# A fused retention and two-MoE kernel: decode scratch and activation sum of the first unit moved into PSUM, scores moved inside the first layer

## Chip, cores and metric

The kernel runs on one NeuronCore of a Trainium2 chip. The metric is device time in microseconds, from the first to the last instruction with what lies around it; three runs of the kernel before gave 1019.86, 1021.78 and 1024.08 us.

## What is computed

Three stages follow each other. A retention layer (4 batches, 8 heads, 768 tokens, head size 64, a decaying state per head) gives 3072 token rows of 512 values. A dense layer follows, and then a routed mixture of 8 experts:

```python
state = gamma * state + k_t v_t^T ;  y_t = scale * q_t state        # retention
h = x @ w_in
g = np.maximum(h, 0.0) + np.log1p(np.exp(-np.abs(h)))               # softplus
x = g @ w_out                                                       # 512 -> 2048 -> 512
e = argmax(x @ w_gate); out = x + prob_e * relu(x @ w1[e]) @ w2[e]  # where x @ w_skip > 0
```

All inputs are float32; `w_in` and `w_out` arrive as 64-bit words (a float64 each), and the kernel turns each word's two halves into one float32 by integer operations.

## The kernel before, in words

TensorE multiplies in a format with fewer bits than float32, so every factor is split into `hi` (rounded) and `lo` (the rest), and each product is three matmuls: hi by hi, lo by hi, hi by lo.

**Units and steps.** The 3072 tokens are 8 units T of 384. A unit has 16 steps f, one for each 128 of the 2048 hidden columns; s = 16 T + f counts all steps. The engines' queues hold the instructions in program order, which the source writes out by hand in the loop at line 748. In step s:

- scores of the next unit's retention, one pair of heads and one chunk of 128 tokens (`attn_a`, L373, TensorE) and their masking (`attn_m`, L379, VectorE);
- `mm1(T, f)` (L518): 12 matmuls, 384 columns each, into one PSUM bank *hp*; there are two such banks, so step s+1 writes the bank of step s-1;
- `act_a(T, f)` on ScalarE: Abs of *hp* (L529), Exp (L530), in unit 0 two Identity passes (L532, L533; in later units one VectorE pass, L543), and Ln (L534); from unit 1 on also a Relu of *hp* (L537);
- `attn_b`: retention sums into the bank *y* (L394, L396), state sums into columns of the bank *wps* (L403), update of the state (L411, VectorE);
- `dec_fin`: for a decoded block, ScalarE copies it to `hi` (L331), SP issues a load of a raw block three further on, POOL subtracts for `lo` (L333);
- `act_p`: two POOL additions (L545, L546);
- `act_hi` of step s-1: VectorE adds (L556 in unit 0, L554 later) to give `g`, ScalarE rounds it to `hi` (L557); one decode pass; `act_lo` of step s-1: VectorE subtracts (L563); again `dec_fin`;
- at the last chunk of a pair of heads, `attn_out` turns *y* into `xth` (L421, ScalarE) and `xtl` (L422, VectorE);
- `mm2` of step s-2 (L575): nine matmuls, 512 columns each, into three accumulators.

**Decode.** The dense weights are 32 blocks (16 of `w_in`, 16 of `w_out`), decoded during unit 0 only. A block takes three VectorE passes over 128x512 words: shift and mask (L312), or in the sign (L316), or in the low half's top bits (L320). `dec(n)` issues the next n passes. Ten blocks are decoded before the steps begin, together with unit 0's own retention; the other 66 passes lie in steps 0 to 15: two in step 0, one in step 1, then 4 and 5 in turn.

**PSUM.** Eight banks: two *hp*, three accumulators, and one each tagged `sc`, `y` and `wps`. In the kernel before, head 0's scores go to `sc` and head 1's to columns 256 to 383 of `wps`.

Of the kernel before, what the change touches and what calls it, by code (L numbers as in the profile page):

```python
# [7 lines left out]
F32 = mybir.dt.float32  # L8
F32R = mybir.dt.float32r
BF16 = mybir.dt.bfloat16  # L10
I32 = mybir.dt.int32
AF = mybir.ActivationFunctionType
ALU = mybir.AluOpType
# [8 lines left out]
TT = 384  # L22
# [3 lines left out]
KD = DM // 128  # L26
# [45 lines left out]
def retention_moe_moe2(ctx: ExitStack, tc: tile.TileContext, a: dict, out: bass.AP):  # L72
    nc = tc.nc
# [9 lines left out]
    ps_s = ctx.enter_context(tc.tile_pool(name="ps_s", bufs=1, space=PSUM))  # L83
# [187 lines left out]
    with tc.manual_schedule():  # L271
        with ExitStack() as p1:
# [3 lines left out]
            at1 = p1.enter_context(tc.tile_pool(name="at1", bufs=1))  # L276
            at2 = p1.enter_context(tc.tile_pool(name="at2", bufs=2))
            gp2 = p1.enter_context(tc.tile_pool(name="gp2", bufs=2))
            mp = p1.enter_context(tc.tile_pool(name="mp", bufs=2))
# [6 lines left out]
            wps = ps_s.tile([128, 512], F32, name="wps")  # L286
# [18 lines left out]
            def decode():  # L305
                for n, (f, side) in enumerate(blocks):
                    w = wo[:, f] if side else wi[:, f].rearrange("p t k n -> p t (k n)")
                    hi, lo = w[:, 0, :], w[:, 1, :]
                    raw = raws[n].rearrange("p (n two) -> p n two", two=2)
                    lw, hw = raw[:, :, 0], raw[:, :, 1]  # L310
                    m = mp.tile([128, 512], I32, name="m")
                    nc.vector.tensor_scalar(  # L312
                        out=m, in0=hw, scalar1=0x07FFFFFF, scalar2=3, op0=ALU.bitwise_and, op1=ALU.logical_shift_left,
                    )
                    yield
                    nc.vector.scalar_tensor_tensor(  # L316
                        out=m, in0=hw, scalar=-0x40000000, in1=m, op0=ALU.bitwise_and, op1=ALU.bitwise_or,
                    )
                    yield
                    nc.vector.scalar_tensor_tensor(  # L320
                        out=m, in0=lw, scalar=29, in1=m, op0=ALU.logical_shift_right, op1=ALU.bitwise_or,
                    )
                    ready.append((m, hi, lo))
                    yield
# [10 lines left out]
            def dec(n):  # L335
                for _ in range(n):
                    next(steps, None)
# [26 lines left out]
            def attn_a(U, p, c, dst=None, am=None):  # L364
                s = st[U, p]
                cs = slice(c * 128, (c + 1) * 128)
                if dst is None:
                    sc = ps_s.tile([128, 512], F32, name="sc")
                    dst = (sc[:, 0:128], wps[:, 256:384])
                    am = at1.tile([128, 256], F32, name="am")  # L370
                for h in range(2):
                    hs = slice(h * 64, (h + 1) * 64)
                    nc.tensor.matmul(dst[h], lhsT=s["kt"][hs, cs], rhs=s["qt"][hs, cs], start=True, stop=True)  # L373
                s["am", c] = am, dst

            def attn_m(U, p, c):
                am, dst = st[U, p]["am", c]
                for h in range(2):
                    nc.vector.scalar_tensor_tensor(  # L379
                        out=am[:, h * 128:(h + 1) * 128], in0=dst[h], scalar=cst[:, C_MS + 2 * p + h:C_MS + 2 * p + h + 1], in1=mask,  # L380
                        op0=ALU.mult, op1=ALU.mult,
                    )

            def attn_b(U, p, c, dw=None):
                s = st[U, p]
                cg = (U % 2) * CPU + c
                cs = slice(c * 128, (c + 1) * 128)
                if dw is None:
                    dw = wps[:, 0:D]
                    if c == 0:  # L390
                        s["y"] = ps_s.tile([128, 512], F32, name="y")[:, 0:TT]
                y, (am, _) = s["y"], s.pop(("am", c))
                if cg:
                    nc.tensor.matmul(y[:, cs], lhsT=wsb[p], rhs=s["qt"][:, cs], start=True, stop=False)  # L394
                for h in range(2):
                    nc.tensor.matmul(  # L396
                        y[h * 64:(h + 1) * 64, cs], lhsT=nat(s["vn"], c, h), rhs=am[:, h * 128:(h + 1) * 128],
                        start=(cg == 0), stop=True,
                    )
                if cg < S // 128 - 1:  # L400
                    for h in range(2):
                        hs = slice(h * 64, (h + 1) * 64)
                        nc.tensor.matmul(dw[hs], lhsT=nat(s["kn"], c, h), rhs=nat(s["vn"], c, h), start=True, stop=True)  # L403
                    for h in range(2):
                        hs = slice(h * 64, (h + 1) * 64)
                        if cg == 0 and U == 0:
                            nc.scalar.activation(out=wsb[p][hs, hs], in_=dw[hs], func=AF.Copy)
                        elif cg == 0:
                            nc.vector.tensor_copy(wsb[p][hs, hs], dw[hs])
                        else:  # L410
                            nc.vector.scalar_tensor_tensor(  # L411
                                out=wsb[p][hs, hs], in0=wsb[p][hs, hs], scalar=cst[hs, C_DEC + p:C_DEC + p + 1], in1=dw[hs],
                                op0=ALU.mult, op1=ALU.add,
                            )
# [11 lines left out]
            seq = [(p, c) for p in range(NP) for c in range(CPU)]  # L426
# [83 lines left out]

            gh, gl = {}, {}

            def mm1(T, f):
                hp = ps_h.tile([128, 512], F32, name="hp")[:, 0:TT]
                n = 0
                for w, x in ((0, xth[T]), (1, xth[T]), (0, xtl[T])):
                    for kk in range(KD):
                        nc.tensor.matmul(  # L518
                            hp, lhsT=wi[:, f, w, kk, :], rhs=x[:, kk, :], start=(n == 0), stop=(n == 3 * KD - 1),
                        )  # L520
                        n += 1
                gl[T, f] = hp

            def act_a(T, f):
                hp = gl[T, f]
                u = gp2.tile([128, TT], F32, name="u")
                ln = gp2.tile([128, TT], F32, name="ln")
                t = at1.tile([128, TT], F32, name="t")
                nc.scalar.activation(out=u, in_=hp, func=AF.Abs)  # L529
                nc.scalar.activation(out=u, in_=u, func=AF.Exp, scale=-1.0)  # L530
                if T == 0:
                    nc.scalar.activation(out=t, in_=u, func=AF.Identity, bias=1.0)  # L532
                    nc.scalar.activation(out=t, in_=t, func=AF.Identity, bias=io8[:, 7:8])  # L533
                nc.scalar.activation(out=ln, in_=u, func=AF.Ln, bias=1.0)  # L534
                g = gp2.tile([128, TT], F32, name="g")
                if T:
                    nc.scalar.activation(out=g, in_=hp, func=AF.Relu)  # L537
                gl[T, f] = u, ln, t, g, hp
# [10 lines left out]
            def act_hi(T, f):  # L549
                g, ln, hp = gl[T, f]  # L550
                hi = gp3.tile([128, TT], F32R, name="hi")
                gl[T, f] = g, ln
                if T:
                    nc.vector.tensor_tensor(out=g, in0=g, in1=ln, op=ALU.add)  # L554
                else:
                    nc.vector.scalar_tensor_tensor(out=g, in0=hp, scalar=0.0, in1=ln, op0=ALU.max, op1=ALU.add)  # L556
                nc.scalar.activation(out=hi, in_=g, func=AF.Copy)  # L557
                gh[T, f] = hi

# [173 lines left out]
            NS = NU * NF  # L733
# [14 lines left out]
            for s in range(NS + 2):  # L748
                T, f = divmod(s, NF)
                U = T + 1  # L750
                i = f - 2 if U < NU and 2 <= f < 2 + len(seq) else None
                if f >= 14 and U + 1 < NU:
                    attn_first(U + 1, f - 14)
                if s == 2 * NF:
                    init_records()
                if s == 1:
                    attn_a(U, *seq[0])
                    attn_m(U, *seq[0])
                if i is not None:
                    if s != 2:  # L760
                        attn_a(U, *seq[i])
                        attn_m(U, *seq[i])
                    if i % CPU == 1 and i + CPU < len(seq):
                        attn_scale_q(U, i // CPU + 1)
                dec(3+s%2 if s > 1 else (2, 0)[s])
                if s < NS:
                    mm1(T, f)
                for fn in todo.get(s + 0.5, []):
                    fn()
                if f == 0 and 1 < U < NU:  # L770
# [46 lines left out]
        with ExitStack() as left:  # L817
# [194 lines left out]
            for m, (ns, nb) in enumerate(PAIRS):  # L1012
                s, b = vis[ns], vis[nb]
# [48 lines left out]
            with tc.For_i(0, nv, 1) as it:  # L1062
                s = {"n": 0, "nb": 4, "xg": xgb[0]}
# [51 lines left out]
```

## Time and profile before

| | |
|---|---|
| median of three runs | 1021.78 us (1019.86 to 1024.08) |
| the profiled execution | 1020.42 us, its span 1018.3 us |
| TensorE busy | 962.4 us (95%) |
| VectorE, ScalarE, POOL busy | 584.7, 482.4, 563.1 us |
| mean granted TensorE clock | 0.97 of full speed |

In the profile PE is TensorE's matmuls, PEld its weight loads, DVE VectorE, ACT ScalarE, SP the engine that issues DMAs. L518 is line 518 of the kernel. A row "out<-in" names the tiles by the program's names. A releaser, after "<-", is what the waiting instruction waited for last.

### The profile page before, as it was taken

The numbers are of one execution on the slowest core, as the hardware profiler recorded it, in microseconds if no ns is written. First come the engines' busy times: TensorE is split into PE (matmuls) and PEld (weight loads), VectorE is DVE, ScalarE is ACT, GpSimd is POOL, SyncE is SP. The second block draws the span as 40 slices with busy tenths as digits, with TensorE's granted clock in tenths as the row PEclk, the third lists the DMA queues.
The fourth block names the chain that finished last, engine by engine and source line by source line (L and its number), as shares of the span: only waits on it lengthen the run. The fifth ranks groups of instructions, "written<-read, shape, count | busy, mean of one in ns | idle before, by whom it ended". The sixth has DMA issues, their size and how long they took to land.

```text
span 1018.3 us, 15594 instructions
## 1 busy us (share of the span) xinstructions
PE 962.4 (95%) x5558; PEld 802.9 (79%) x5558; DVE 584.7 (57%) x1260; ACT 482.4 (47%) x915; POOL 563.1 (55%) x455
## 2 busy tenths in 40 slices
PE   7888989999999999999999999999797999999994
PEld 6667768888888888888888888888685878797883
DVE  6899995455444644544454454446435375556743
ACT  1265565455354544544553554455453365354640
POOL 4567776545645654555465365446462673546642
PEclk8699999999999999999999999999897999999998
DMA  8535342112111212111121112001027294557710
GB/s 284 182 94 172 123 136 88 37 32 99 45 55 32 94 32 62 64 56 39 32 93 40 55 63 63 1 1 63 1 82 270 76 346 144 216 165 240 248 66 20
DMA packets 59424, 102.15 MB, mean 100 GB/s; under 512 B 9026, under 2 KB 35810, under 8 KB 59344
## 3 DMA queue, kind: packets, MB, share of 16 engines
q1 hardware_dynamic: 54432, 90.57, 26.9%
q0 software_dynamic: 4048, 8.85, 2.5%
q10 hardware_dynamic: 864, 1.70, 0.4%
q8 instruction: 45, 0.74, 0.3%
q14 instruction: 35, 0.29, 0.1%
HBM read 85.18 MB, written 17.85 MB: 101 GB/s over the span
## 4 chain that ended last, share of the span: by engine, by line
PE 80%; DVE 12%; issue 4%; ACT 2%; DMA 1%; POOL 1%; SPq 0%; ACTq 0%; POOLq 0%; DVEq 0%
PE hp L518 25%; PE ac L575 24%; PE op L902 9%; PE hp L862 8%; DVE m L316 3%; PE sc L373 3%; PE y L396 3%; PE hp L876 2%; DVE m L312 2%; DVE m L320 1%; PE y L394 1%; DVE lo L563 1%; PE tp L600 1%; PE hp L172 1%; DVE wsb L411 1%
## 5 line engine op out<-in xcount | busy, mean ns | idle before, releaser
L545 POOL TENSOR_TENSOR ln<-ln,t 128x384 f32<-128x384 f32 x127 | 151.4, 1192 | 255.6 <-ACT ln L534 125.9
L575 PE MATMUL ac<-wo,hi 128*128 128x512 f32 x768 | 272.5, 409 | 6.1 <-ACT hi L557 6.1
L518 PE MATMUL hp<-xth,wi 128*128 128x384 f32 x1024 | 215.5, 353 | 9.2 <-DVE g L556 8.4
L518 PEld LDWEIGHTS hp<-xth,wi 128*128 128x128 f32 x1024 | 177.6, 190 | 23.4 <-DVE g L556 10.2
L529 ACT ACTIVATE u<-hp 128x384 f32<-128x384 f32 x128 | 62.7, 490 | 250.3 <-PE hp L518 234.3
L575 PEld LDWEIGHTS ac<-wo,hi 128*128 128x128 f32 x768 | 145.1, 189 | 43.8 <-ACT hi L557 7.2
L546 POOL TENSOR_TENSOR ln<-ln,u 128x384 f32<-128x384 f32 x127 | 152.8, 1204 | 10.0
L575 PE MATMUL ac<-wo,lo 128*128 128x512 f32 x384 | 151.8, 395 | 0.8 <-DVE lo L563 0.7
L563 DVE TENSOR_TENSOR lo<-g,hi 128x384 fp32r<-128x384 f32 x128 | 97.5, 762 | 68.2 <-ACT hi L557 67.0
L518 PE MATMUL hp<-xtl,wi 128*128 128x384 f32 x512 | 112.8, 342 | 0.0
L156 POOL TENSOR_TENSOR l<-raw,h 128x1024 fp32r<-128x1024 f32 x30 | 77.3, 2588 | 54.7 <-ACT h L153 32.1
L543 DVE TENSOR_SCALAR t<-u 128x384 f32<-128x384 f32 x112 | 44.0, 393 | 98.2 <-ACT u L530 95.7
L411 DVE SCALAR_TENSOR_TENSOR wsb<-wsb,cst,wps 64x64 f32<-64x64 f32 x128 | 35.8, 279 | 102.9 <-PE wps L403 101.9
L518 PEld LDWEIGHTS hp<-xtl,wi 128*128 128x128 f32 x512 | 93.2, 191 | 0.0
L156 DVE TENSOR_TENSOR l<-raw,h 128x1024 fp32r<-128x1024 f32 x42 | 77.1, 1863 | 14.3 <-ACT h L153 13.8
L575 PEld LDWEIGHTS ac<-wo,lo 128*128 128x128 f32 x384 | 72.8, 190 | 14.0 <-DVE lo L563 2.6
L557 ACT ACTIVATE hi<-g 128x384 fp32r<-128x384 f32 x128 | 67.1, 524 | 34.3 <-DVE g L554 17.6
L153 ACT ACTIVATE h<-raw 128x1024 fp32r<-128x1024 f32 x71 | 72.7, 1057 | 10.0 <-PE hp L876 3.9
L530 ACT ACTIVATE u<-u 128x384 f32<-128x384 f32 x128 | 67.2, 525 | 4.1
L534 ACT ACTIVATE ln<-u 128x384 f32<-128x384 f32 x128 | 67.2, 525 | 3.5
L554 DVE TENSOR_TENSOR g<-g,ln 128x384 f32<-128x384 f32 x112 | 61.8, 552 | 0.9 <-POOL ln L546 0.9
L902 PE MATMUL op<-h,gh 128*128 128x512 f32 x152 | 59.9, 394 | 0.0
(200 smaller groups left out, 1545.6 us busy)
## 6 DMA issues: line engine op xcount, KB each, us to landing
raw<-in_moe_w SPq DMA_DIRECT2D x72, 512.0 KB
raw<-in_moe_w_out SPq DMA_DIRECT2D x16, 512.0 KB
raw<-in_moe_w_in SPq DMA_DIRECT2D x15, 512.0 KB
kn<-in_qkv SPq DMA_DIRECT2D x32, 192.0 KB
vn<-in_qkv SPq DMA_DIRECT2D x32, 192.0 KB
kt<-in_qkv SPq DMA_DIRECT2D x31, 192.0 KB
qt<-in_qkv SPq DMA_DIRECT2D x31, 192.0 KB
x1d<-x SPq DMA_DIRECT2D x21, 256.0 KB
```

The lines of the kernel that those rows point to most:

```text
L153: nc.scalar.activation(out=h, in_=r, func=AF.Copy)
L156: eng.tensor_tensor(out=lo, in0=r, in1=h.bitcast(F32), op=ALU.subtract)
L518: nc.tensor.matmul(hp, lhsT=wi[:, f, w, kk, :], rhs=x[:, kk, :], start=(n == 0), stop=(n == 3 * KD - 1),)
L530: nc.scalar.activation(out=u, in_=u, func=AF.Exp, scale=-1.0)
L534: nc.scalar.activation(out=ln, in_=u, func=AF.Ln, bias=1.0)
L545: eng.tensor_tensor(out=ln, in0=ln, in1=t, op=ALU.subtract)
L546: eng.tensor_tensor(out=ln, in0=ln, in1=u, op=ALU.add)
L557: nc.scalar.activation(out=hi, in_=g, func=AF.Copy)
L563: nc.vector.tensor_tensor(out=lo, in0=g, in1=gh[T, f].bitcast(F32), op=ALU.subtract)
L575: nc.tensor.matmul(ac[T, j], lhsT=x[:, js], rhs=wo[:, f, w, :], start=(f == 0 and n == 0), stop=(f == NF - 1 and n == 2),)
L862: nc.tensor.matmul(hp2[(2 * i + g) % 4][:, 0:w], lhsT=wt[:, kk, g * 128:(g + 1) * 128], rhs=x[:, kk, 0:w], start=(n == 0 and kk == 0), sto ...
L902: nc.tensor.matmul(op, lhsT=s[x][:, f, js], rhs=s[w, f // 2][:, f % 2, :], start=(f == 0 and n == 0), stop=(f == NF2 - 1 and n == 2),)
```

## The change

In the first two passes of a decode the words lie in the PSUM bank `sc` (new tile `x`); only the third pass writes the SBUF tile `m`. In unit 0 the sum `g` is written over *hp* in its bank, and `hi` and `lo` read it from there. While unit 0 is worked on, head 0's scores go to the columns of `wps` that head 1's had, and head 1's to columns 384 to 511 of the bank of `y`, which is claimed with the scores; their matmuls are issued after the eighth of the twelve matmuls of `mm1`, and the masking after all twelve. The decode passes of a step are dealt out anew: two before `mm1`, one or two behind it (three in step 0, none in step 1), one between `act_hi` and `act_lo`.

```diff
@@ -308,17 +308,18 @@
                     hi, lo = w[:, 0, :], w[:, 1, :]
                     raw = raws[n].rearrange("p (n two) -> p n two", two=2)
                     lw, hw = raw[:, :, 0], raw[:, :, 1]
-                    m = mp.tile([128, 512], I32, name="m")
+                    x = ps_s.tile([128, 512], I32, name="mx", tag="sc")
                     nc.vector.tensor_scalar(
-                        out=m, in0=hw, scalar1=0x07FFFFFF, scalar2=3, op0=ALU.bitwise_and, op1=ALU.logical_shift_left,
+                        out=x, in0=hw, scalar1=0x07FFFFFF, scalar2=3, op0=ALU.bitwise_and, op1=ALU.logical_shift_left,
                     )
                     yield
                     nc.vector.scalar_tensor_tensor(
-                        out=m, in0=hw, scalar=-0x40000000, in1=m, op0=ALU.bitwise_and, op1=ALU.bitwise_or,
+                        out=x, in0=hw, scalar=-0x40000000, in1=x, op0=ALU.bitwise_and, op1=ALU.bitwise_or,
                     )
                     yield
+                    m = mp.tile([128, 512], I32, name="m")
                     nc.vector.scalar_tensor_tensor(
-                        out=m, in0=lw, scalar=29, in1=m, op0=ALU.logical_shift_right, op1=ALU.bitwise_or,
+                        out=m, in0=lw, scalar=29, in1=x, op0=ALU.logical_shift_right, op1=ALU.bitwise_or,
                     )
                     ready.append((m, hi, lo))
                     yield
@@ -364,6 +365,12 @@
             def attn_a(U, p, c, dst=None, am=None):
                 s = st[U, p]
                 cs = slice(c * 128, (c + 1) * 128)
+                if U == 1:
+                    if c == 0:
+                        s["yt"] = ps_s.tile([128, 512], F32, name="y")
+                        s["y"] = s["yt"][:, 0:TT]
+                    dst = (wps[:, 256:384], s["yt"][:, 384:512])
+                    am = at1.tile([128, 256], F32, name="am")
                 if dst is None:
                     sc = ps_s.tile([128, 512], F32, name="sc")
                     dst = (sc[:, 0:128], wps[:, 256:384])
@@ -387,7 +394,7 @@
                 cs = slice(c * 128, (c + 1) * 128)
                 if dw is None:
                     dw = wps[:, 0:D]
-                    if c == 0:
+                    if c == 0 and U != 1:
                         s["y"] = ps_s.tile([128, 512], F32, name="y")[:, 0:TT]
                 y, (am, _) = s["y"], s.pop(("am", c))
                 if cg:
@@ -510,7 +517,7 @@
 
             gh, gl = {}, {}
 
-            def mm1(T, f):
+            def mm1(T, f, mid=None):
                 hp = ps_h.tile([128, 512], F32, name="hp")[:, 0:TT]
                 n = 0
                 for w, x in ((0, xth[T]), (1, xth[T]), (0, xtl[T])):
@@ -519,6 +526,8 @@
                             hp, lhsT=wi[:, f, w, kk, :], rhs=x[:, kk, :], start=(n == 0), stop=(n == 3 * KD - 1),
                         )
                         n += 1
+                        if n == 2 * KD and mid is not None:
+                            mid()
                 gl[T, f] = hp
 
             def act_a(T, f):
@@ -532,7 +541,7 @@
                     nc.scalar.activation(out=t, in_=u, func=AF.Identity, bias=1.0)
                     nc.scalar.activation(out=t, in_=t, func=AF.Identity, bias=io8[:, 7:8])
                 nc.scalar.activation(out=ln, in_=u, func=AF.Ln, bias=1.0)
-                g = gp2.tile([128, TT], F32, name="g")
+                g = gp2.tile([128, TT], F32, name="g") if T else hp
                 if T:
                     nc.scalar.activation(out=g, in_=hp, func=AF.Relu)
                 gl[T, f] = u, ln, t, g, hp
@@ -553,7 +562,7 @@
                 if T:
                     nc.vector.tensor_tensor(out=g, in0=g, in1=ln, op=ALU.add)
                 else:
-                    nc.vector.scalar_tensor_tensor(out=g, in0=hp, scalar=0.0, in1=ln, op0=ALU.max, op1=ALU.add)
+                    nc.vector.scalar_tensor_tensor(out=g, in0=g, scalar=0.0, in1=ln, op0=ALU.max, op1=ALU.add)
                 nc.scalar.activation(out=hi, in_=g, func=AF.Copy)
                 gh[T, f] = hi
 
@@ -753,18 +762,22 @@
                     attn_first(U + 1, f - 14)
                 if s == 2 * NF:
                     init_records()
-                if s == 1:
-                    attn_a(U, *seq[0])
-                    attn_m(U, *seq[0])
+                mid = seq[0 if s == 1 else i] if s == 1 or T == 0 and s > 2 and i is not None else None
                 if i is not None:
-                    if s != 2:
+                    if T:
                         attn_a(U, *seq[i])
                         attn_m(U, *seq[i])
                     if i % CPU == 1 and i + CPU < len(seq):
                         attn_scale_q(U, i // CPU + 1)
-                dec(3+s%2 if s > 1 else (2, 0)[s])
-                if s < NS:
+                if T == 0:
+                    dec(2)
+                if mid is not None:
+                    mm1(T, f, lambda: attn_a(U, *mid))
+                    attn_m(U, *mid)
+                elif s < NS:
                     mm1(T, f)
+                if T == 0:
+                    dec(1 + s % 2 if s > 1 else (3, 0)[s])
                 for fn in todo.get(s + 0.5, []):
                     fn()
                 if f == 0 and 1 < U < NU:
```

## Rows read from the trace of the kernel before

**Rows 1.** the page's slices of the span: VectorE, tenths busy:

```profile
DVE  6899995455444644544454454446435375556743
```

**Rows 2.** busy time by stretches: us busy, (x) instructions, granted clock, DMA:

```profile
100.00:125.00 25.00, 22.59 (x123) 17.40 (x121) 24.28 (x38) 14.29 (x28) 18.29 (x15) 1.00 0.42 133
```

**Rows 3.** chain of waits from 45 to 157 us, shares by line:

```profile
by line: DVE m L316 19.9%; issue 16.6%; DVE m L312 13.1%; DVE lo L563 11.4%; DVE m L320 9.3%; PE hp L518 5.6%; DVE am L379 5.4%; DVE g L556 4.9%; DVE wsb L411 3.7%; PE ac L575 1.9%; DVE xtl L422 1.8%; ACT hi L557 1.5%; ACT wo L331 1.1%; ACT
```

**Rows 4.** VectorE by line, 45 to 157 us: count, busy us, mean ns, idle before:

```profile
L320 DVE SCALAR_TENSOR_TENSOR m<-raw,m 128x512 int32<-128x512 int32 x23 | 24.2, 1050 | 0.5
L316 DVE SCALAR_TENSOR_TENSOR m<-raw,m 128x512 int32<-128x512 int32 x23 | 24.1, 1048 | 0.5
L563 DVE TENSOR_TENSOR lo<-g,hi 128x384 fp32r<-128x384 f32 x15 | 19.9, 1326 | 1.4 <-ACT hi L557 1.4
L312 DVE TENSOR_SCALAR m<-raw 128x512 int32<-128x512 int32 x23 | 17.4, 757 | 0.0
L556 DVE SCALAR_TENSOR_TENSOR g<-hp,ln 128x384 f32<-128x384 f32 x16 | 8.8, 553 | 0.2
```

**Rows 5.** timeline, POOL and VectorE: start us, us long, engine, line:

```profile
104.64 1.19 POOL L545 TENSOR_TENSOR ln<-ln,t 128x384 f32<-128x384 f32 x1
...
104.89 1.37 DVE L563 TENSOR_TENSOR lo<-g,hi 128x384 fp32r<-128x384 f32 x1
```

**Rows 6.** instructions of L312 and L316, whole span: ns min/median/max, first and last start:

```profile
L312 DVE TENSOR_SCALAR m<-raw x32: 410/456/1479, 7.8 to 149.1; 128x512 int32<-128x512 int32 x32
...
L316 DVE SCALAR_TENSOR_TENSOR m<-raw,m x32: 674/965/1670, 8.4 to 150.4; 128x512 int32<-128x512 int32 x32
```

**Rows 7.** instructions of L422, whole span:

```profile
L422 DVE TENSOR_TENSOR xtl<-y,xth x30: 543/546/558, 22.5 to 668.3; 128x384 fp32r<-128x384 f32 x30
```

**Rows 8.** timeline, ScalarE:

```profile
57.58 0.49 ACT L529 ACTIVATE u<-hp 128x384 f32<-128x384 f32 x1 [1.54 <-PE hp L518]
...
60.21 0.62 ACT L331 ACTIVATE wo<-m 128x512 fp32r<-128x512 f32 x1
...
64.25 0.49 ACT L529 ACTIVATE u<-hp 128x384 f32<-128x384 f32 x1 [2.45 <-PE hp L518]
...
133.91 0.49 ACT L529 ACTIVATE u<-hp 128x384 f32<-128x384 f32 x1 [1.98 <-PE hp L518]
...
143.98 0.63 ACT L331 ACTIVATE wo<-m 128x512 fp32r<-128x512 f32 x1 [1.16 <-DVE m L320]
144.52 0.51 ACT L557 ACTIVATE hi<-g 128x384 fp32r<-128x384 f32 x1
...
148.54 0.49 ACT L529 ACTIVATE u<-hp 128x384 f32<-128x384 f32 x1 [3.52 <-PE hp L518]
...
159.40 0.49 ACT L529 ACTIVATE u<-hp 128x384 f32<-128x384 f32 x1 [2.26 <-PE hp L518]
```

**Rows 9.** timeline of step 9, TensorE and ScalarE:

```profile
103.79 1.68 PE L518 MATMUL hp<-xth,wi 128*128 128x384 f32 x8
...
106.26 0.49 ACT L529 ACTIVATE u<-hp 128x384 f32<-128x384 f32 x1 [1.97 <-PE hp L518]
```

**Rows 10.** chain of waits in the second unit: start us, us:

```profile
161.39 0.30 PE sc L373
...
161.81 2.31 PE hp L518 x12
...
173.01 2.32 PE hp L518 x12
```

**Rows 11.** VectorE by line, before the steps (0 to 45 us):

```profile
L316 DVE SCALAR_TENSOR_TENSOR m<-raw,m 128x512 int32<-128x512 int32 x9 | 10.6, 1174 | 0.3
```

**Rows 12.** timeline, TensorE:

```profile
54.55 1.71 PE L518 MATMUL hp<-xth,wi 128*128 128x384 f32 x8 [2.19 <-DVE g L556]
...
144.56 2.69 PE L518 MATMUL hp<-xth,wi 128*128 128x384 f32 x8 [2.04 <-DVE g L556]
```

**Rows 13.** busy time by stretches, around the later gap:

```profile
146.00:148.00 2.00, 2.00 (x7) 2.00 (x7) 1.97 (x3) 0.00 (x0) 1.92 (x2) 0.50 0.13 47
```

## The prediction, made before any run of the change

> **What bounds the kernel now.** I read the slices of the page first. VectorE stands at 9 tenths from about 75 to 150 us and at 4 to 6 over most of the rest [rows 1]. The change touches little but the first unit (16 steps, about 45 to 157 us), so I went there with the stretches: of 25 us VectorE is busy 24.28, TensorE 22.59, ScalarE 14.29, POOL 18.29, and the granted clock is full [rows 2]. The chain of waits says the same: between 45 and 157 us most of the path is VectorE's decoding (L312, L316, L320), L563 and its other passes; TensorE's L518 has 5.6% [rows 3]. VectorE bounds this unit.
>
> Why it is so full is in the groups of VectorE by line. The three decode passes and `lo` take 757 to 1326 ns on average, while L556, which has one input in PSUM and one in SBUF, takes 553 [rows 4]. The timeline shows what stretches them: L563 begins at 104.89, in the middle of a POOL addition (104.64 to 105.83), and ends 0.43 us after it, having taken 1.37 us [rows 5]. Left alone, an L316 takes 0.674, its minimum [rows 6], and an L422, a subtraction of the same size as L563 but with one input in PSUM, takes 543 to 558 in all of its 30 instances, beside POOL or not [rows 7]. Waiting for POOL is the extra time, and it falls on passes with two SBUF inputs and on L312.
>
> **What the change takes from VectorE.** `x` in PSUM leaves L316 and L320 one SBUF input; `g` in PSUM does the same for L563. Priced as L316's minimum and as L422: 23 L316 save 0.37 each, 8.6 us; 23 L320 likewise 8.6; 15 L563 save 0.78 each, 11.7. L556 stays at 553, its output merely going to PSUM. L312 keeps its SBUF input but writes PSUM, which no row shows: its own extremes, 0.410 and 1.479 [rows 6], are the bounds, and I leave it at its mean of 757 since POOL is unchanged. VectorE so drops by about 29 us: at 24.28 of 25 [rows 2] it had some 109 us in the unit's 112, now 80, or 5.0 us for each of 16 steps. If it set the pace, that would be a large gain.
>
> **What takes its place.** The step is bound to the *hp* bank. There are two, so `mm1(s+1)` writes the one that step s-1 used. Before, the last reader of that bank was `g` of step s-1 (L556). Now `g` lies in the bank, and the last readers are `hi` (L557, ScalarE) and then `lo` (L563, VectorE). ScalarE works in order, and `hi` of s-1 is issued behind the whole of `act_a(s)`, which waits for the end of `mm1(s)`, and behind one decode copy. So a loop closes: mm1(s), five activations, a copy, `hi`, `lo`, mm1(s+1). Its length comes from rows, counted from the start of Abs (L529):
> - Abs to the copy: 57.58 to 60.21, 2.63 us [rows 8];
> - copy to `hi`: 143.98 to 144.52, 0.54 [rows 8]; `hi` itself 0.51;
> - `lo` as L422: 0.55 [rows 7]. mm1(s+1) can begin 4.23 us after Abs(s);
> - mm1 to the next Abs: 103.79 to 106.26, 2.47 [rows 9];
> - the scores, now in the middle of mm1 where they lie inside this loop: from L373 to L518, 161.39 to 161.81, 0.42 [rows 10].
>
> The loop is 7.12 us. Before, Abs runs from 64.25 (step 3) to 133.91 (step 13), 6.97 a step [rows 8]. What is late next is thus ScalarE's order. VectorE hides inside: per step some 5.0 us against 7.12, its decode passes done while the activations run.
>
> *The moved parts* I cost at nothing else. The 66 decode passes stay 66, two ahead of mm1, one or two behind it, one between `g` and `lo`; one copy stands ahead of `hi` in every step to 14, the second of the even steps behind it. The scores no longer wait for the state update L411 of the step before. Head 1's share `y`'s bank now: at the first chunk of a pair (steps 5, 8, 11) they wait for L422 of the step before, which follows `hi`, at times a copy, and `xth`, and should end some 1.2 us into mm1, when the scores come about 1.6 in (8 of 12 matmuls in 2.47 [rows 9]); 0 to 0.3 us if not. Behind L379, which follows two decode passes, the attention sums and `mm2` are queued on TensorE. By the busy share that leaves about 0.7 us to spare ahead of mm1(s+1): attention 1.2 and mm2 2.3 in 4.23. POOL's decode subtraction and two additions, some 1.2 to 1.3 each (one is 1.19 [rows 5]), follow the copy of s-1 and end about when Abs(s) starts; `hi` needs `g` three us later. SP's raw loads follow the copy as before.
>
> **The sum**, against the profiled execution's own time of 1020.42 us (its span is 1018.3), which is 1.36 under the median of 1021.78:
> - *Before the steps* (to 45 us): 9 L316 at 1174 ns [rows 11] could save 0.50 each, 4.4 us. ScalarE, TensorE and POOL are also on this path, so the bounds are 0 and 4.4; I take -2.0. The Trainium skill (VectorE: DVE Perf Modes, "Why PSUM operands drop a tier") says that a PSUM operand holds an fp32 pass to one element per cycle; an L312 would then be as slow as a lone L316, by that page an estimate of up to 0.28 more for each of the ten here, and the sum would be up to 2.8 us higher. No run so far shows it.
> - *Steps 0 to 2*: mm1(2) started at 54.55 after a gap of 2.19, waiting for `g` [rows 12]. mm1(1) had ended at 52.36; with Abs(1) some 0.4 behind that, because a decode copy is now in front of it, plus 4.23, mm1(2) starts at about 57.0: +2.4. At the least `hi` and `lo` come on top, +1.1. A longer gap also costs clock: after 2.04 us without work, mm1(15) ran from 144.56 to its Abs at 148.54, 3.98 instead of 2.47 [rows 8, 12], at a granted 0.50, the lower of the two levels, 1.2 against 2.4 GHz [rows 13]. Here mm1(2) took 3.03 already, so between -0.6 and +0.95; I take +0.5. Together +2.9.
> - *Step 2 to 3*: 57.58 to 64.25 is 6.67 [rows 8], now 7.12: +0.45.
> - *Steps 3 to 13*: ten times 7.12 against 69.66: +1.6.
> - *Steps 13 to 17*: 133.91 to 159.40, 25.49 [rows 8]. Now 6.70 and 6.70 (no scores), 6.16 (no copy), and about 5.5 where the next unit leaves two activations out: 25.06. TensorE has gaps of some 2 us here, as the one that lost the clock, so I put one loss of 1.5 in again: +1.1.
>
> Sum: -2.0 + 2.9 + 0.45 + 1.6 + 1.1 = **+4.0**. From step 17 on TensorE's own work sets the steps [rows 10], and nothing there is changed, so the shift stays to the end. Against the median: 1021.78 + 4.0 = **1025.8 us**, 0.4% up. A measurement of this kernel tells about 0.5%, 5.1 us, from no change, so the likeliest outcome is no clear difference, leaning to slower: 29 us of VectorE are freed and a longer hand-over eats them.
>
> **Rivals.**
> *A, VectorE's relief sets the pace (faster).* If the bank's later release were hidden, TensorE would bound the unit as it does the next one, where mm1 runs from 161.81 to 173.01 in two steps, 5.6 each [rows 10]. Eleven steps at 1.37 less give -15, and with the start's 2.0 about 1005. For it: the 24.28 of 25. Against: ScalarE's order in the rows leaves `hi` no way ahead of act_a(s). 0.08.
> *B, the clock falls inside the steps (slower).* TensorE's waits, now spread over the step, become one gap in front of each mm1. I work out 0.7 us, and as much in a step was idle at full clock before (2.41 of 25 us [rows 2]), but a gap of 2 us cost the clock [rows 12, 13]. If attention and mm2 finish earlier than I think, or the loop is longer, mm1 runs at half clock: 1.5 us a time. Four to six falls give +10 to +13, 1032 to 1035. [...] 0.15.
> *C, the change does not relieve VectorE.* Decode passes in PSUM still wait for POOL, or take longer there. Then VectorE (7 us a step) and the loop meet, and `lo` is late: 0.3 to 0.6 us a step, +3 to +7 on top, 1029 to 1033. Against: L556 and L422 never stretched [rows 4, 7]. 0.15.
> Forecast: 0.62.
>
> **How the numbers follow.** With all terms at their better ends (start -4.4, steps 0 to 2 at +1.1, no lost clock) the sum is -1.7 or 1020; a reading 1.5 us lower from the spread of the runs gives the low end, 1018.5. With the start at 0, mm1(2) at half clock, one more loss and 0.3 a step for late passes it is near +11, 1033; B's upper part lies a little over, so 1034. A and the top of B are left out. Of the forecast's 0.62, some 0.40 lies within 0.5% and 0.22 over it; B is slower, C split about evenly. That gives faster 0.08, same 0.48, slower 0.44.
>
> **What would show it.** Right: L316, L320 and L563 near 0.69 and 0.55 with VectorE well under 20 of 25 us, and yet Abs every 7.1 us; L518 waiting for L563 and no longer for L556; ScalarE without pause from Abs to `hi`. The scores would cost 0.42 inside mm1. Wrong: Abs every 6 us or less with TensorE full (A); granted clock at 0.5 between 60 and 135 us (B); L316 still over 0.9 (C). L312 near 0.69 would shrink the gain of the start.

## The result, and the profile after

The changed kernel takes 1027.60 us (median of six runs, 1026.27 to 1028.65) against 1022.42 of six runs of the kernel before. The ratio is 1.0054, with a 95% interval of 1.0035 to 1.0073: 5.2 us slower, 1.8 us over the forecast of 1025.8, and inside its range. The interval reaches to both sides of the 0.5% (5.1 us) that the prediction took as the line to no clear difference; that the two kernels are equally fast lies outside it. The profiled execution took 1028.46 us, its span 1026.3.

The line numbers move in the changed kernel: L518 is L525 (mm1), L320 is L321, L529 is L538 (Abs), L331 is L332 (decode copy), L556 is L565 (sum), L557 is L566 (`hi`), L563 is L572 (`lo`), L373 is L380 (scores), L379 is L386 (masks), L422 is L429 (`xtl`), L545 and L546 are L554 and L555.

The slices of the page: VectorE in tenths busy, and the granted clock:

```profile
DVE  5876763545544554554464454446434375556743
...
PEclk7689999999999999999999999999897999999997
```

VectorE's row of nines is gone [rows 1]; over the same slices, about 51 to 154 us, it stands at 6 and 7. The same stretch as in [rows 2] says what came in its place:

```profile
100.00:125.00 25.00, 19.62 (x109) 14.69 (x107) 16.11 (x33) 14.19 (x30) 13.66 (x14) 1.00 0.47 157
```

Of 25 us VectorE is busy 16.11 where it was 24.28, but TensorE is down as well, 19.62 where it was 22.59. VectorE by line, 45 to 157 us:

```profile
L316 DVE SCALAR_TENSOR_TENSOR mx<-raw,mx 128x512 int32<-128x512 int32 x23 | 15.9, 689 | 0.3
L321 DVE SCALAR_TENSOR_TENSOR m<-raw,mx 128x512 int32<-128x512 int32 x23 | 15.6, 680 | 0.3
L312 DVE TENSOR_SCALAR mx<-raw 128x512 int32<-128x512 int32 x22 | 15.2, 692 | 0.5
L565 DVE SCALAR_TENSOR_TENSOR hp<-hp,ln 128x384 f32<-128x384 f32 x15 | 8.4, 563 | 2.7 <-POOL ln L555 2.5
L572 DVE TENSOR_TENSOR lo<-hp,hi 128x384 fp32r<-128x384 f32 x14 | 7.8, 558 | 18.2 <-ACT hi L566 18.2
```

L316 and L321 are at 689 and 680 ns where they were 1048 and 1050, `lo` is at 558 where it was 1326 [rows 4]: the relief came as priced. Over the whole first unit every L316 takes 682 to 697 ns, every L321 674 to 689 and every `lo` 557 to 559, so not one is stretched beside POOL. L565, which writes into its own PSUM input, hardly changed (563 against 553). The chain of waits, shares by line (as [rows 3]):

```profile
by line: PE hp L525 39.2%; ACT t L542 7.2%; DVE lo L572 7.1%; ACT u L538 6.3%; ACT t L541 6.2%; ACT u L539 6.2%; ACT ln L543 4.8%; ACT hi L566 4.5%; PE wps L380 4.4%; issue 4.0%; ACT wo L332 3.2%; ACT wi L332 2.8%; DVE mx L312 0.6%; DVE m L
```

VectorE's decoding has all but left the path. mm1 now has 39.2%, and the five activations, the copies and `hi` stand on it one after the other. The waits from 60 to 150 us (who waited for whom: total us, times, longest):

```profile
DVE lo L572 <- ACT hi L566: 15.7, 12, 2.4
PE hp L525 <- DVE lo L572: 15.7, 12, 1.5
```

mm1 waits for `lo` in 12 steps, and `lo` for `hi`; in the same stretch of the kernel before, mm1 waited for the sum, 4.6 us in 5 steps. One turn of the loop in the timeline, step 9 to step 10:

```profile
110.45 1.68 PE L525 MATMUL hp<-xth,wi 128*128 128x384 f32 x8 [1.33 <-DVE lo L572]
...
112.06 0.37 PE L380 MATMUL wps<-qt,kt 64*128 64x128 f32 x1
...
112.48 0.97 PE L525 MATMUL hp<-xtl,wi 128*128 128x384 f32 x4
...
113.54 0.49 ACT L538 ACTIVATE u<-hp 128x384 f32<-128x384 f32 x1 [3.22 <-PE hp L525]
...
116.18 0.61 ACT L332 ACTIVATE wo<-m 128x512 fp32r<-128x512 f32 x1
116.70 0.47 ACT L566 ACTIVATE hi<-hp 128x384 fp32r<-128x384 f32 x1
...
117.20 0.56 DVE L572 TENSOR_TENSOR lo<-hp,hi 128x384 fp32r<-128x384 f32 x1 [1.02 <-ACT hi L566]
...
117.81 0.44 PE L525 MATMUL hp<-xth,wi 128*128 128x384 f32 x1 [1.33 <-DVE lo L572]
```

mm1 begins at 110.45; after eight matmuls, at 112.06, the scores; Abs at 113.54; the copy at 116.18, 2.64 later; `hi` 0.52 behind it; `lo` at 117.20; and mm1 of the next step at 117.81, within 0.1 of `lo`'s end. From Abs to mm1 it is 4.27 us, and 4.23 had been worked out. The starts of Abs for steps 0, 2, 3, 13 and 17:

```profile
49.35 0.49 ACT L538 ACTIVATE u<-hp 128x384 f32<-128x384 f32 x1 [0.90 <-PE hp L525]
...
62.02 0.49 ACT L538 ACTIVATE u<-hp 128x384 f32<-128x384 f32 x1 [4.89 <-PE hp L525]
...
69.38 0.49 ACT L538 ACTIVATE u<-hp 128x384 f32<-128x384 f32 x1 [3.21 <-PE hp L525]
...
143.01 0.49 ACT L538 ACTIVATE u<-hp 128x384 f32<-128x384 f32 x1 [3.22 <-PE hp L525]
...
167.25 0.49 ACT L538 ACTIVATE u<-hp 128x384 f32<-128x384 f32 x1 [1.99 <-PE hp L525]
```

Steps 3 to 13 take 73.63 us, 7.36 each, where they took 6.97 [rows 8], and step 17 comes at 167.25, 7.85 later than at 159.40. That is nearly the whole difference of the two spans (8.0). The medians differ by less, 5.2, since this profiled execution lies 0.9 over its median and that of before 2.0 under the median of its six runs.

### The profile page after: what moved, and what is told of

It reads as the page before. It is cut to its first block, busy times and chain, and to the rows that moved or that the text cites. A ratio compares the mean times of both kernels' runs of the same rounds, so it can differ in the third digit from the quotient of the medians.

```text
span 1026.3 us, 15610 instructions
## 1 busy us (share of the span) xinstructions
PE 961.4 (94%) x5558; PEld 800.8 (78%) x5558; DVE 554.9 (54%) x1260; ACT 479.2 (47%) x915; POOL 546.4 (53%) x455
## 4 chain that ended last, share of the span: by engine, by line
PE 84%; ACT 6%; DVE 4%; issue 2%; DMA 2%; POOL 1%; ACTq 0%; POOLq 0%; DVEq 0%; SPq 0%
PE hp L525 28%; PE ac L584 23%; PE op L915 9%; PE hp L875 8%; PE sc L380 3%; PE y L403 3%; PE hp L889 2%; PE y L401 1%; PE tp L609 1%; ACT u L539 1%; DVE lo L572 1%; PE hp L172 1%; ACT u L538 1%; ACT t L542 1%; PE wps L410 1%
## 5 line engine op out<-in xcount | busy, mean ns | idle before, releaser
L554 POOL TENSOR_TENSOR ln<-ln,t 128x384 f32<-128x384 f32 x127 | 146.3, 1152 | 254.5 <-ACT ln L543 124.7
L525 PE MATMUL hp<-xth,wi 128*128 128x384 f32 x1024 | 215.9, 353 | 25.2 <-DVE lo L572 25.1
L525 PEld LDWEIGHTS hp<-xth,wi 128*128 128x128 f32 x1024 | 178.1, 191 | 42.3 <-DVE lo L572 31.4
L538 ACT ACTIVATE u<-hp 128x384 f32<-128x384 f32 x128 | 62.9, 491 | 277.8 <-PE hp L525 256.8
L555 POOL TENSOR_TENSOR ln<-ln,u 128x384 f32<-128x384 f32 x127 | 149.2, 1175 | 10.0
L525 PE MATMUL hp<-xtl,wi 128*128 128x384 f32 x512 | 113.7, 344 | 0.0
L572 DVE TENSOR_TENSOR lo<-g,hi 128x384 fp32r<-128x384 f32 x112 | 77.0, 688 | 66.2 <-ACT hi L566 66.2
L525 PEld LDWEIGHTS hp<-xtl,wi 128*128 128x128 f32 x512 | 92.1, 190 | 1.4
L566 ACT ACTIVATE hi<-g 128x384 fp32r<-128x384 f32 x112 | 58.8, 525 | 25.3 <-DVE g L563 17.9
L563 DVE TENSOR_TENSOR g<-g,ln 128x384 f32<-128x384 f32 x112 | 61.7, 551 | 0.9 <-POOL ln L555 0.9
```

The lines of the kernel that those rows point to most:

```text
L525: nc.tensor.matmul(hp, lhsT=wi[:, f, w, kk, :], rhs=x[:, kk, :], start=(n == 0), stop=(n == 3 * KD - 1),)
L554: eng.tensor_tensor(out=ln, in0=ln, in1=t, op=ALU.subtract)
L555: eng.tensor_tensor(out=ln, in0=ln, in1=u, op=ALU.add)
L572: nc.vector.tensor_tensor(out=lo, in0=g, in1=gh[T, f].bitcast(F32), op=ALU.subtract)
```

## The experiments

Theory L is that of the prediction: the loop mm1, five activations, decode copy, `hi`, `lo`, mm1 through the two *hp* banks sets the step. Theory S puts the cost down to the scores inside mm1, theory D to the decoding in PSUM. All runs have the kernel before beside them (medians 1021.89 to 1022.06). Edits are against the changed kernel unless said otherwise.

**e1: the sum back in SBUF.**

```diff
-                g = gp2.tile([128, TT], F32, name="g") if T else hp
+                g = gp2.tile([128, TT], F32, name="g")
...
-                    nc.vector.scalar_tensor_tensor(out=g, in0=g, scalar=0.0, in1=ln, op0=ALU.max, op1=ALU.add)
+                    nc.vector.scalar_tensor_tensor(out=g, in0=hp, scalar=0.0, in1=ln, op0=ALU.max, op1=ALU.add)
```

> The changed kernel with one part undone: unit 0's sum g goes to an SBUF tile again, so the last reader of an hp bank is the sum (L565) and no longer lo (L572). Theory L (the loop mm1, five activations, copy, hi, lo, mm1 through the hp bank sets the step): the loop is gone, VectorE bounds the step again with relieved decode passes: 4.5 decode passes at 0.69, masks 0.7, state 0.6, sum 0.56, lo some 1.3 beside POOL, xtl 0.2, about 6.4 us a step instead of 7.36 in steps 3 to 13. Eleven steps save 10.5 us and the first steps 2 to 4: 1012 to 1016 us, faster than the kernel before. Theory S (the scores inside the first layer cost the time): nothing changes in the step, 7.3 us, about 1027 us. Theory D (decoding in PSUM costs more than it saves): VectorE stays full and the time stays over 1022 us.

Measured: 1014.81 us, 0.9927 of the kernel before (0.9905 to 0.9949), 12.8 under the changed kernel. One part of three, undone, turns a loss into a gain; S and D fall. `lo` in VectorE's groups by line, 45 to 150 us:

```profile
L572 DVE TENSOR_TENSOR lo<-g,hi 128x384 fp32r<-128x384 f32 x15 | 18.9, 1262 | 11.4 <-ACT hi L566 11.4
```

`lo` is stretched beside POOL again, 1262 ns, and still the kernel is faster. The time went otherwise than I had put it, though. Abs of steps 2, 3, 13 and 17:

```profile
57.29 0.49 ACT L538 ACTIVATE u<-hp 128x384 f32<-128x384 f32 x1 [3.74 <-PE hp L525]
...
63.34 0.49 ACT L538 ACTIVATE u<-hp 128x384 f32<-128x384 f32 x1 [1.86 <-PE hp L525]
...
132.04 0.49 ACT L538 ACTIVATE u<-hp 128x384 f32<-128x384 f32 x1 [1.59 <-PE hp L525]
...
153.19 0.49 ACT L538 ACTIVATE u<-hp 128x384 f32<-128x384 f32 x1 [0.87 <-PE hp L525]
```

Steps 3 to 13 take 6.87 each, not 6.4. Step 2 comes at 57.29 where it was 62.02, but 3.80 of these 4.73 us stand at Abs of step 0 already (45.55 against 49.35), which no edit of e1 touches: that is a difference between two executions. From Abs of step 0 to Abs of step 17 it is 107.64 us against 117.90, so 10.3 us are the edit's in these two: 0.9 in steps 0 to 2, 1.3 from step 2 to 3, 4.9 in steps 3 to 13, 3.1 in the last four (21.15 us, not 24.24). The total was right, the split was not. What bounds the middle steps of e1 (VectorE is busy 21.3 of 25 us, the attention sums wait for masks in nine steps, the granted clock means 0.93 in two stretches) was not taken apart.

**e2: the decode copy taken out of the loop.**

```diff
                     attn_b(U, *seq[i])
-                dec_fin()
...
                     act_hi(*divmod(s - 1, NF))
+                    dec_fin()
```

> The changed kernel, g still in the hp bank, but the decode copies of a step (ScalarE L332 with its load and its POOL subtraction) are issued behind hi of the step before instead of ahead of it. Theory L: the copy is a link of the loop, 0.52 us from its start to that of hi; Abs follows Abs every 6.84 us in steps 3 to 13 instead of 7.36, and with steps 2 and 14 the time falls by 6 to 7 us to about 1021 us. Theory S or D: ScalarE is no part of the bound, nothing changes, 1027 us.

Measured: 1021.28 us, 0.9992 (0.9982 to 1.0002), 6.3 under the changed kernel. Abs of steps 3 and 13:

```profile
67.97 0.49 ACT L538 ACTIVATE u<-hp 128x384 f32<-128x384 f32 x1 [2.70 <-PE hp L525]
...
136.42 0.49 ACT L538 ACTIVATE u<-hp 128x384 f32<-128x384 f32 x1 [2.70 <-PE hp L525]
```

68.45 us for ten steps, 6.845 each; 6.84 was expected. The place of one ScalarE copy takes 0.52 us, its whole link, off every step, on an engine that is busy little more than half of the time (14.19 of 25 us in the changed kernel). This is the run that shows the loop.

**e3: the scores ahead of mm1 again**, in their new banks.

```diff
                 if mid is not None:
-                    mm1(T, f, lambda: attn_a(U, *mid))
-                    attn_m(U, *mid)
-                elif s < NS:
+                    attn_a(U, *mid)
+                if s < NS:
                     mm1(T, f)
+                if mid is not None:
+                    attn_m(U, *mid)
```

> The changed kernel, but the scores are issued ahead of mm1 as in the kernel before (their banks stay wps and y, the masks stay behind mm1). Theory L: in front of mm1 TensorE waits 1.3 to 1.45 us for lo, so the scores fit there and leave the loop: mm1 to Abs falls from 3.10 to 2.47, Abs every 6.7 to 6.8 us, 6 to 7 us less, about 1021 us, as no more than a second term. Theory S: the scores are the whole cause, the kernel falls below the one before, 1015 us or less. Theory D: no change, 1027 us.

Measured: 1028.50 us, 1.0072 (1.0054 to 1.0089). A miss. Ordinary steps did fall to 6.74 us, as theory L has it, but three of them, at the first chunk of a pair of heads, take 9.55, 8.77 and 8.06. TensorE's timeline in the first of these:

```profile
79.46 0.79 PE L380 MATMUL y<-qt,kt 64*128 64x128 f32 x2 [1.98 <-DVE xtl L429]
80.19 2.88 PE L525 MATMUL hp<-xth,wi 128*128 128x384 f32 x8
```

Head 1's scores wait 1.98 us for L429, which still reads the bank of `y`, and behind them mm1 waits, in TensorE's own order. Then its eight matmuls take 2.88 us instead of 1.68; the stretch has the clock at half:

```profile
80.00:82.00 2.00, 2.00 (x8) 1.82 (x7) 1.93 (x6) 0.00 (x0) 2.00 (x2) 0.50 0.25 89
```

The prediction had this wait at 0 to 0.3 us for scores inside mm1, and there it is hidden; ahead of mm1 it is bare. The third of the long steps waits 1.98 us as well (at 124.78) and keeps the clock: it takes 8.06 us against 6.75, so the wait alone costs 1.3 us, and the other 1.5 of the first are the clock's.

**e4: the sum in the bank alone**, on the kernel before.

```diff
-                g = gp2.tile([128, TT], F32, name="g")
+                g = gp2.tile([128, TT], F32, name="g") if T else hp
...
-                    nc.vector.scalar_tensor_tensor(out=g, in0=hp, scalar=0.0, in1=ln, op0=ALU.max, op1=ALU.add)
+                    nc.vector.scalar_tensor_tensor(out=g, in0=g, scalar=0.0, in1=ln, op0=ALU.max, op1=ALU.add)
```

> The kernel before with one part of the change alone: unit 0's sum g written over hp in its bank; decoding and scores as before. Theory L: L563 falls from 1.33 to 0.56 us, but mm1 of the next step now waits for lo: loop 4.26 + 2.47 = 6.7 us a step where one copy stands ahead of hi, 7.2 where two do, and decode passes still stretched by POOL fill VectorE: 6.7 to 7.0 us a step, within 4 us of the kernel before (1018 to 1026 us), TensorE waiting for lo (L563) and not for the sum. Theory S or D: this part only relieves VectorE by 0.77 us a step and the time falls by 10 us or more to 1012 us.

Measured: 1029.07 us, 1.0067 (1.0055 to 1.0080). S and D, which saw only relief, are out by 17 us; L, which allowed up to 1026, is out by 3. Many steps take 6.74, as the loop has it. The long ones show why it is worse than that:

```profile
71.55 1.35 DVE L320 SCALAR_TENSOR_TENSOR m<-raw,m 128x512 int32<-128x512 int32 x1
...
72.82 0.55 DVE L563 TENSOR_TENSOR lo<-hp,hi 128x384 fp32r<-128x384 f32 x1
...
73.42 2.93 PE L518 MATMUL hp<-xth,wi 128*128 128x384 f32 x8 [1.96 <-DVE lo L563]
```

A decode pass between the sum and `lo` waits for POOL (1.35 us), `lo` comes late, mm1 waits 1.96 us, and its eight matmuls then take 2.93 us at half clock. That is the prediction's rival B, not in the changed kernel but here.

**e5: scores inside mm1 only where the bank of `y` asks for it.**

```diff
-                if mid is not None:
+                if mid is not None and mid[1]:
+                    attn_a(U, *mid)
+                if mid is not None and not mid[1]:
                     mm1(T, f, lambda: attn_a(U, *mid))
-                    attn_m(U, *mid)
                 elif s < NS:
                     mm1(T, f)
+                if mid is not None:
+                    attn_m(U, *mid)
```

> The changed kernel; the scores stay inside mm1 only at the first chunk of a pair (steps 1, 5, 8 and 11), where the bank of y is still being read, and go ahead of mm1 in the other eight steps. Theory L with the bank of y as a second wait: the eight steps take 6.75 us as in the run with all scores ahead, the others 7.36, no step waits for xtl (L429) and none loses the clock; 8 times 0.61 less than the changed kernel, 5 us, about 1022 to 1023 us. Theory M (scores ahead of mm1 cost clock or order in themselves, not through the bank of y): long steps of 8 us and more stay, 1027 us or more.

Measured: 1021.93 us, 0.9998 (0.9987 to 1.0008), 5.7 under the changed kernel. Abs of steps 3 to 6, of which step 5 is a first chunk:

```profile
67.09 0.49 ACT L538 ACTIVATE u<-hp 128x384 f32<-128x384 f32 x1 [2.60 <-POOL ln L555]
...
73.84 0.49 ACT L538 ACTIVATE u<-hp 128x384 f32<-128x384 f32 x1 [3.13 <-POOL ln L555]
...
81.20 0.49 ACT L538 ACTIVATE u<-hp 128x384 f32<-128x384 f32 x1 [2.83 <-PE hp L525]
...
87.94 0.49 ACT L538 ACTIVATE u<-hp 128x384 f32<-128x384 f32 x1 [3.13 <-POOL ln L555]
```

6.75, 7.36, 6.74 us. The releaser named is POOL's L555, which ended at 67.03; mm1 ended at 66.99, and Abs follows it by 0.10 us as in the changed kernel, so POOL is at most level with mm1 here. Inside the loop the scores cost 0.61 us a step, and the wait of e3 was the bank of `y`.

**e6 and e7: `hi` and `lo` ahead of the activations**; e6 with the sum in the bank, e7 with it in SBUF (as in e1).

```diff
+                if 1 <= s <= NF:
+                    act_hi(*divmod(s - 1, NF))
+                    dec(1)
+                    act_lo(*divmod(s - 1, NF))
                 if s < NS:
                     act_a(T, f)
                 if i is not None:
                     attn_b(U, *seq[i])
-                dec_fin()
                 if s < NS:
                     act_p(T, f)
+                dec_fin()
...
-                if 1 <= s <= NS:
+                if NF < s <= NS:
                     act_hi(*divmod(s - 1, NF))
```

> The changed kernel with all three parts kept; only the order of issue in unit 0 is changed: hi and lo of step s-1 ahead of the five activations of step s, and the decode copies behind POOL's two additions. Theory L: mm1 of step s+1 then waits for a lo that no longer stands behind act_a(s); the loop is open and TensorE bounds the step: mm1 with scores 3.10, then attention and mm2 2.94, about 6.0 to 6.3 us instead of 7.36. Eleven steps save 12 to 15 us, the first and last ones 3 to 6 more: 1006 to 1014 us, under both kernels. Theory R (the sum in the bank is bad in itself, because a bank is held for too long whatever the order): over 1020 us.

> The order of issue of the run before this one, but unit 0's sum g in SBUF. It tells what the sum in the bank is worth once the order does not close the loop. Theory L: lo has two SBUF inputs again and waits for POOL, some 0.5 to 0.8 us of VectorE a step; where TensorE bounds at about 6.1 us VectorE then stands at 6.0 to 6.4, so 0 to 5 us slower than that run, 1008 to 1016 us. Theory R: clearly faster than that run, by 5 us or more.

Measured: 1028.02 us, 1.0063 (1.0043 to 1.0082), and 1031.88, 1.0081 (1.0059 to 1.0103). Both lie more than 10 us over what was expected, and e7 is no faster than e6, so the bank is not the reason. The waits of e6:

```profile
ACT hi L566 <- DVE hp L565: 41.5, 12, 4.3
...
DVE am L386 <- PE y L380: 9.0, 8, 2.6
...
DVE m L321 <- POOL wi L334: 4.0, 4, 1.9
```

`hi` waits for the sum 41.5 us in 12 steps. On VectorE I had left the sum of step s-1 behind the masks, which wait for scores in the middle of mm1(s), and behind decode passes, which wait for POOL to let `m` go. The timeline of one step:

```profile
111.91 0.97 PE L525 MATMUL hp<-xtl,wi 128*128 128x384 f32 x4
...
114.30 0.56 DVE L565 SCALAR_TENSOR_TENSOR hp<-hp,ln 128x384 f32<-128x384 f32 x1
...
114.89 0.49 ACT L566 ACTIVATE hi<-hp 128x384 fp32r<-128x384 f32 x1 [4.33 <-DVE hp L565]
...
115.28 0.49 ACT L538 ACTIVATE u<-hp 128x384 f32<-128x384 f32 x1
```

mm1 has ended by 112.9; the sum runs at 114.30, `hi` at 114.89, and Abs of the finished bank only at 115.28. One loop was opened and another closed, through VectorE's order.

**e8 and e9: the same, with the sum right behind the masks** (e8 in the bank, e9 in SBUF). On top of the edit of e6:

```diff
-                if T == 0:
-                    dec(1 + s % 2 if s > 1 else (3, 0)[s])
+                if T == 0 and s == 0:
+                    dec(3)
...
                     act_p(T, f)
+                if T == 0 and s > 1:
+                    dec(1 + s % 2)
                 dec_fin()
```

> The changed kernel with all three parts kept; hi and lo of step s-1 stand ahead of the five activations of step s, as in e6, but on VectorE the sum of step s-1 comes right behind the masks, and the one or two decode passes that stood between go behind the state update. Theory L with e6's reading (there the sum of s-1 waited behind the masks, which wait for the scores inside mm1(s), and behind decode passes which wait for POOL's use of m, so that hi held Abs(s) back by some 2 us): the sum is done about when mm1(s) ends, Abs(s) is held by 0.5 us at most, steps of 6.2 to 6.6 us: 1009 to 1017 us. Theory R (a sum that stays in the bank costs over 5 us whatever the order): over 1020 us.

> The order of e8 with unit 0's sum g in SBUF. Theory L: the bank no longer decides in this order, and lo with two SBUF inputs waits for POOL, 0.5 to 0.8 us of VectorE a step: 0 to 6 us slower than e8, 1010 to 1020 us. Theory R: faster than e8 by 5 us or more.

Measured: 1018.26 us, 0.9961 (0.9948 to 0.9974), and 1017.95, 0.9953 (0.9937 to 0.9969). e8 keeps all three parts of the change and differs from it in nothing but the order of issue: 9.3 us faster than the changed kernel, and 3.6 faster than the one before. Abs of steps 3 and 13 in e8:

```profile
66.83 0.49 ACT L538 ACTIVATE u<-hp 128x384 f32<-128x384 f32 x1
...
132.27 0.49 ACT L538 ACTIVATE u<-hp 128x384 f32<-128x384 f32 x1
```

65.44 us, 6.54 a step as expected, though the whole is 1.3 us over its range. And in this order the place of the sum no longer matters: e9 and e8 are alike, where in the order of the changed kernel it decides 12.8 us (e1). It was the bank together with the order, not the bank alone.

**e10: e1 and e5 together**, the sum in SBUF, scores inside mm1 at first chunks only; its edits are the two shown there.

> The decode part with neither cost of the others: g in SBUF (e1), and the scores inside mm1 only at the first chunk of a pair (e5). In e1 VectorE is busy 21.3 of 25 us and the attention sums wait for the masks 0.4 to 1.2 us in most steps, since the masks follow the scores late. Theory L: scores ahead of mm1 give the masks earlier and shorten mm1 by 0.6 in eight steps; between none of it (VectorE bounds) and all of it (5 us): 1009 to 1015 us. If scores ahead of mm1 now wait for the state update of the step before, as they did in the kernel before, 1015 to 1018 us.

Measured: 1013.84 us, 0.9925 (0.9912 to 0.9938), 1.0 under e1, less than the runs of the two can tell apart. It and e1 beat the kernel before by 0.7%; e8 and e9 beat it by 0.4 to 0.5%. From 100 to 125 us TensorE is busy 22.85 of 25 us and VectorE 21.70: both fuller than in the changed kernel (19.62 and 16.11).

## Why the prediction was right, point by point

*What VectorE is relieved of* was right to a few per cent: 0.36 us a pass for L316, 0.37 for L320, 0.77 for `lo`, against 0.37, 0.37 and 0.78. Rival C is out.

*The loop* was right as a mechanism, and its ScalarE half to 0.04 us; e2 takes one link out and gets the link's length back, and e8 opens it by order alone. Rival A is out in the changed kernel. It was not baseless: with the loop gone (e1, e10) VectorE's relief does show, though as 7 to 8 us and not 17.

*The scores in mm1* were under-sized, 0.42 against 0.61 to 0.62. In step 9 of the kernel before, whose first eight matmuls begin at 103.79 [rows 9], the last four follow at 105.30:

```profile
105.30 0.86 PE L518 MATMUL hp<-xtl,wi 128*128 128x384 f32 x4
```

So they start 1.51 us into mm1, and Abs comes 0.96 later; in the turn shown above it is 2.03 and 1.06. The scores themselves took what was priced (112.06 to 112.48, 0.42), but they start 1.61 us into mm1, 0.10 after the place of the last four, and Abs comes 0.10 later behind these. A stretch that starts with the scores [rows 10] doesn't show either. That is 0.2 a step, 2.2 us in eleven.

*The sum, term by term.* By the medians its end is 1.2 us off (+5.2 against +4.0), its terms by more:

| term | forecast | measured (profiled executions) |
|---|---|---|
| before the steps, to Abs of step 0 | -2.0 | -0.3 |
| steps 0 to 2 | +2.9 | +4.75 |
| step 2 to 3 | +0.45 | +0.7 |
| steps 3 to 13 | +1.6 | +4.0 |
| steps 13 to 17 | +1.1 | -1.25 |
| sum | +4.0 | +7.85 (medians: +5.2) |

That they make up a sum so near is in part luck: steps 0 to 13 were sized 4.5 us too low, and steps 13 to 17 2.35 too high.

*Before the steps* about half of the gain of L316 was given back by L312. L312 before the change, from 0 to 45 us, and then the first two passes after it:

```profile
L312 DVE TENSOR_SCALAR m<-raw 128x512 int32<-128x512 int32 x10 | 4.8, 480 | 6.0 <-DMA raw<-in_moe_w_in 6.0
```

```profile
L312 DVE TENSOR_SCALAR mx<-raw 128x512 int32<-128x512 int32 x10 | 6.9, 691 | 7.4 <-DMA raw<-in_moe_w_in 7.1 <-DMA raw<-in_moe_w_out 0.2
L316 DVE SCALAR_TENSOR_TENSOR mx<-raw,mx 128x512 int32<-128x512 int32 x9 | 6.3, 696 | 0.3
```

L316 falls from 1174 to 696 ns, 4.3 us over nine, but the ten L312 take 691, as long as an L316, where they took 480 and the shortest 410. This is what the rule cited in the prediction makes of it (the Trainium skill, VectorE: DVE Perf Modes, "Why PSUM operands drop a tier"): the trace agrees. Ten times 691 against 480 is 2.1 us, half of those 4.3. The -0.3 of the table belongs to one pair of executions. Up to Abs of step 0 every version but e4 runs the changed kernel's instructions, and e4 those of the kernel before: Abs comes at 49.66 and 50.31 in the two profiles with the old decoding, and at 45.55 to 49.35, median 47.5, in the ten with the new one, the changed kernel's own being the latest. By these the start gained about 2.5 us, near the -2.0 that was forecast, and with it the terms add up to about +5.7, close to the +5.2 of the medians.

*Steps 0 to 2*: I had priced the copy ahead of Abs(1), but not what POOL then does with it. Its subtraction starts at 52.62, and VectorE's second addition of step 0, with two SBUF inputs, waits for it:

```profile
52.62 1.27 POOL L334 TENSOR_TENSOR wi<-m,wi 128x512 fp32r<-128x512 f32 x1 [2.81 <-ACT wi L332]
52.65 1.65 DVE L555 TENSOR_TENSOR ln<-ln,u 128x384 f32<-128x384 f32 x1
...
56.65 0.49 ACT L566 ACTIVATE hi<-hp 128x384 fp32r<-128x384 f32 x1 [1.00 <-DVE hp L565]
...
57.78 2.93 PE L525 MATMUL hp<-xth,wi 128*128 128x384 f32 x8 [5.40 <-DVE lo L572]
```

1.65 us instead of 0.56. Behind it VectorE still has two decode passes of step 1 ahead of the sum, so `hi` waits 1.00 us for the sum, which the prediction had ready in time. mm1(2) starts after a gap of 5.40 us, and runs at half clock throughout: 2.93 us for eight matmuls.

*Steps 13 to 17*: I had put in one loss of clock, 1.5 us, as before. None came, though TensorE paused 2.30 us ahead of mm1(15). Most of the rest is the last of the four steps, 4.52 us and not 5.5.

Rival B did not happen: from 65 to 165 us the granted clock is full. But its condition came about: attention and mm2 took 3.0 us (113.45 to 116.48 in the turn above), not 3.5, and the gaps ahead of mm1 were 1.3 to 1.5 us in steps 4 to 14, about twice the 0.7 that I had worked out, and 2.30 in step 15. By the prediction's own reasoning it was luck that the clock held.

## What to carry to other kernels

Where a result is written back into the buffer that its input came in, ask who reads it last, and where that reader stands in its engine's order: a shorter instruction on the busiest engine was paid for with a loop through an engine that is half idle. When an engine is relieved and the time does not fall, look at what the next producer now waits for, and move issue order before moving data. The gain that is left can be had by keeping the part that relieves and undoing the part that holds the buffer (e1).

## What the hardware showed that I had not expected

A pause of TensorE is a poor sign of its clock by itself. One of 2.30 us ahead of mm1(15) in the changed kernel cost nothing: eight matmuls in 1.68 us, and a full granted clock to 165 us. One of 2.04 in the kernel before, and ones of 1.98 in e3 and 1.96 in e4, were followed by eight matmuls in 2.69 to 2.93 us. Yet another of 1.98 in e3 (ahead of 125.20) and one of 2.04 in e4 (ahead of 111.97) were followed by eight in 1.68, with the clock full behind them. One of 2.19 ahead of mm1(2) in the kernel before lies between: its eight took 1.71 us [rows 12], its last four 1.48 instead of 0.86, at a granted clock of 0.51 from 56 to 58 us:

```profile
56.06 1.48 PE L518 MATMUL hp<-xtl,wi 128*128 128x384 f32 x4
```

Which it will be was not settled here.

A VectorE pass from SBUF with its output in PSUM (L312) ran at 691 ns against a shortest 410 to SBUF, but was no longer stretched beside POOL (682 to 696 ns in all 32 instances, 410 to 1479 before): its mean in the steps fell all the same, from 757 to 692.
